# Fusing an attention block with a feed-forward block: values of two pairs of heads in one TensorE visit, and another order of accumulators at a group's start

## The chip, the cores and the metric

The kernel runs on one core of one Trainium2 chip. The metric is the device time of one execution in microseconds; lower is better. A second profiled execution, recorded by the hardware profiler, gives the rows shown here.

## The reference, cut to what matters

Attention over 4 batches, 8 heads, 768 positions and 64 dimensions per head, with a mask (the first 8 keys and the last 96), a distance bias, and a softmax; its output, 3072 rows of 512, goes through two dense layers with an ELU between them, all in float32:

```
scores = scale * q @ k.T + bias; scores = where(keep, scores, -1e9)
a = softmax(scores);  x = a @ v            # per head
h = x @ w_in;  g = where(h > 0, h, exp(min(h, 0)) - 1)
out = g @ w_out
```

## The kernel before

The 3072 rows are worked in 12 groups of 256 rows (two tiles of 128). Heads go in pairs: hp = 0 to 3 are the four pairs of a group, one head on each half of the 128 partitions. To keep float32 accuracy, most products are made of a rounded high part and a low rest (HI and LO), so that one product is three.

Groups 0 to 2 (n < GS = 3) work in an older way while weights arrive. From group 3 on ("later groups", about 204 us to the end) a group takes four **periods** of about 13.2 us, and TensorE's order in them is written by hand (`seq`, L70 on: operations with it go in that order and no other). One period is:

- two **ups** (L780): first-layer products of 24 matmuls each, 128x128 weights and 256 moving columns, into one PSUM bank per up. ScalarE and VectorE then compute the ELU in three steps (L708, L709, L710) and write `gg`, high and low.
- a **values visit** (L585): for one pair of heads of the *next* group, the product of the transposed probabilities `pt` with the values `rv`, into a tile `pv`: 8 products (6 in a sequence's first group) of 64 rows or columns. The trace has two records for each, so 16 or 12. ScalarE copies `pv` to `xh` high (L323), VectorE subtracts to get the low part (L331), 256 columns each.
- the **odd down** (L840): 21 second-layer products of the previous period's second up, into four accumulators a0 to a3. The second layer is worked by a seven-product scheme on 2 by 2 blocks, so a down has 7 products, each made of three.
- a **visit** (L562, L542): transposes of the next pair's probabilities into two banks `t` and `th` (t0, v0), and the scores of the pair after that into two banks (s0, s1).
- the **even down** (L840): 21 products of this period's first up.

Values of pair hp stand in period hp of the group before their own. `pv` may take bank v0 or t0, the same banks that the transposes of the visit need. The ups, the scores and so the ELU share the banks s0 and s1. `pt` of later groups has one buffer (pts: pt0), `rv` has two (part0, part1), each filled by a DMA on SyncE's queue, on which the first-layer weights `w0s` (four per period) are fetched too.

Between groups, the first accumulators of the new group need the four that the old one leaves, which ScalarE and VectorE combine (L856 to L862, tile `fin`). That happens in period 0 of the new group: odd down of the old group's last product, the visit, then the new group's first down (c = 0). Its 21 products run in the order raw high (a0, a0, a1), sums high (a1, a2, a2, a3), then the low ones.

The orders of ScalarE, VectorE and SyncE come from a planner (`Plan.order`) that places each operation by costs and due times.

Of the kernel before, what the change touches and what calls it, by code (L numbers as in the profile page):

```python
# [16 lines left out]
P = 128  # L17
# [5 lines left out]
NT = 2  # L23
W = NT * P
BIG = float(2 ** 100)

HI, LO = 0, 1
# [228 lines left out]
def pe(cols):  # L256
    return (("PE", cols * 0.47, False),)


def act(n, psum=False, extra=0.0):  # L260
    return (("ACT", (55 if psum else 97) + 0.834 * n + extra, False),)


def dve(n, fast=False, port=False):
    return (("DVE", (75 + 0.521 * n) if fast else (70 + 1.042 * n), fast or port),)
# [10 lines left out]
class Kernel:  # L276
# [191 lines left out]
    def pair(self, b, gi, hp, xh, xl, due, ahead, step, X):  # L468
        nc, p = self.nc, self.plan
# [7 lines left out]
        rv = rqv if rows else self.sb("rv", "rv", [P, VC])  # L477
# [29 lines left out]
        v32 = lambda: rv.t[:, nq if rows else 0:].rearrange("p (t j d) -> p t j d", t=2 * NT, j=2)  # L507
        k32 = lambda: rk.t
        sc = self.scale.t[:, hp:hp + 1]
        if rows:  # L510
# [5 lines left out]
            pv = self.bank("pv", "pv", [P, NT, P], X.get("pv"))  # L516
            self.pair32(b, hp, t0, q32, k32, v32, rqv, rk, pv, due, step, X)
            pvs = lambda: pv.t.rearrange("p i w -> p (i w)")
# [15 lines left out]
        st = self.sb("st", "st", [P, 3, 2 * NT])  # L534
        tiles = [(t0 + i, i * (NG + P)) + self.blocks(t0 + i) for i in range(NT)]
# [28 lines left out]
        def rest():  # L564
            pt = self.sb("pts", "pt", [P, 2, 2 * NT, P])
            d = due - 6000
            for x, tp in enumerate(tps):
                r = slice(64 * x, 64 * x + 64)
                if t0:
                    cut = [(slice(0, HK), slice(0, 4))]  # L570
                else:
                    cut = [(slice(0, kr), slice(2 * i + a0, 2 * i + 2)) for i, (_, _, _, a0, kr, _) in enumerate(tiles)]
                for rows, c in cut:
                    n = (c.stop - c.start) * 128
                    src = lambda tp=tp, rows=rows, c=c: tp.t.rearrange("p (j c) w -> p j c w", j=2)[rows, :, c]
                    out = lambda rows=rows, c=c, r=r: pt.t[rows, :, c, r]
                    p.add(act(n, True) + dve(n), lambda e, src=src, out=out: self.copy(e, out(), src()), [tp], [pt], d + 2 * x)
            pv = self.bank("pv", "pv", [P, NT, P])
            head = [slice(0, 64), slice(64, 128)]

            def values(e):
                for i, (_, _, _, a0, kr, _) in enumerate(tiles):
                    for a in range(a0, 2):
                        for j in range(2):
                            nc.tensor.matmul(pv.t[head[j], i], v32()[:kr, 2 * i + a, j], pt.t[:kr, j, 2 * i + a], start=a == a0, stop=a == 1)  # L585

            n = sum(2 - x[3] for x in tiles)
            self.after = [p.add((("PE", 160 + 216.0 * n, False),), values, [rv, pt], [pv], due, seq=due)]
            pvs = lambda: pv.t.rearrange("p i w -> p (i w)")
            p.add(act(W, True), lambda e: self.copy(e, xh.t[:, HI, hp], pvs()), [pv], [xh], due + 100)  # L590
            p.add(dve(W), lambda e: self.minus(e, xh.t[:, LO, hp], pvs(), xh.t[:, HI, hp]), [pv, xh], [xl], due + 200)

        self.prev = transposes, [v for x in prs for v in x], tps, 53.0 * 2 * sum(2 - x[3] for x in tiles), rest

# [190 lines left out]
    def moe7(self, rows, xh, xl, up_at, down_at):  # L785

        nc, p, N7, DM = self.nc, self.plan, self.NF7, self.DM
# [33 lines left out]
        def down(c, d, gg, low):  # L821
            a, b, ta, tb, k = self.seven[c]
            if not acc:
                acc.extend(self.bank(f"a{i}", "a", [P, 2, half], [s]) for i, s in enumerate(("o0", "o1", "h0", "h1")))
            far = slice(half, DM)
            near_, far_ = lambda w: lambda s: w.t[:, s, near], lambda w: lambda s: w.t[:, s, far]
            parts = ((A22, lambda s: tb.t[:, 2 * s + k], 0, 0), (A11, near_(a), 0, 1), (A12, near_(b), 1, 1), (S2, lambda s: ta.t[:, 2 * s + 1], 1, 0),
                     (S1, lambda s: ta.t[:, 2 * s], 2, 0), (S3, far_(a), 2, 1), (S4, far_(b), 3, 0))
            raw, sums = (0, 1, 2), (3, 4, 5, 6)
            high, rest = ((HI, HI), (HI, LO)), ((LO, HI),)  # L830
            if c < N7 - 1:
                todo = ((raw, high), (sums, high), (raw, rest), (sums, rest))
            else:
                todo = tuple((x, high + rest) for x in ((0, 1), (2, 3), (4, 5), (6,)))

            def products(e, ks, xs):
                for n in ks:
                    g, w, i, j = parts[n]
                    for x, s in xs:
                        nc.tensor.matmul(acc[i].t[:, j], gg.t[:, x, g], w(s), start=c == x == s == 0 and n in (0, 2, 4, 6),  # L840
                                         stop=c == N7 - 1 and x == LO and n in (1, 3, 5, 6))

            for m, (ks, xs) in enumerate(todo):
                need = [low[n] for n, kind in enumerate((raw, sums)) if rest[0] in xs and set(ks) & set(kind)]
                p.add(pe(len(xs) * len(ks) * half), lambda e, ks=ks, xs=xs: products(e, ks, xs), [a, b, ta, tb, gg] + need,
                      [acc[i] for i in sorted({parts[n][2] for n in ks})], d + 10 * m, seq=d + 10 * m)

        for c in range(N7):
            down(c, down_at[c], *up(c, up_at[c]))
        e = down_at[-1] - 20000  # L850
        fin = self.sb("fin", "fin", [P, 8, half], slots=["xh2"])
        first, second, spare, upper, lower = (p.tile(None, x, None) for x in ("first", "second", "spare", "upper", "lower"))
        f = lambda k, n=1: fin.t[:, k:k + n].rearrange("p i w -> p (i w)")
        v = nc.vector.tensor_tensor
# [12 lines left out]
    def build(self):  # L867
# [9 lines left out]
        at, start, wdue, dues = self.T0, {}, {}, []  # L877
# [9 lines left out]
            dues.append(d)  # L887
        self.start = start[self.GS]
        todo, self.held, self.parted, self.loads, self.asked = [], [], [], [], []
        self.prev, self.after = ((lambda: None), [], [], 0.0, (lambda: None)), []  # L890
        last = 0.0
        for n, (b, gi) in enumerate(groups):
# [5 lines left out]
            st = (hi - lo) / (4 * self.NP)  # L898
            for hp in range(self.NP):
# [5 lines left out]
                if n > self.GS:  # L905
                    ahead = start[self.GS] + self.PERIOD * (4 * (n - self.GS - 1) + hp - 2) + self.VISIT
                    d, st = ahead + self.AFTER, 600.0
# [30 lines left out]
        for _, f in sorted(todo, key=lambda x: x[0]):  # L938
# [18 lines left out]
    WARM, FILL = True, 60000.0  # L957
    SLOTS = {"rqv": ["rqv0"], "rk": ["rk0"], "qs": ["qs0"], "ks": ["ks0"], "rv": ["part0", "part1"],
             "s": ["s0", "s1"], "t": ["t0"], "th": ["v0"], "pv": ["v0", "t0"], "h": ["h0", "h1"], "S": ["s0", "s1"], "g7": ["io0", "io1", "io2", "io3"], "ring": ["w012", "w013", "w014", "w015"], "gg": ["gg0", "gg1"], "z": ["z0", "vd0"], "o0": ["o0"], "o1": ["o1"],
             "pr": ["pr0", "pr1", "pr2", "pr3"], "st": [f"st{i}" for i in range(6)], "pt": ["pt0", "pt1"], "pts": ["pt0"],  # L960
             "xh": ["xh0", "xh1", "xh2"], "e": ["z0", "e1"], "gh": ["gg0", "gg1", "gh2"],
             "gl": ["gl0", "gl1", "gl2"], "io": ["io0", "io1", "io2", "io3"], "part": ["part0", "part1", "vd0"]}

# [278 lines left out]
```

## Time and profile before

| | |
|---|---|
| time, median of 3 runs | 678.62 us (678.48 to 679.86) |
| profiled execution, own time | 678.11 us |
| its span | 676.3 us |
| TensorE busy | 660.5 us (98%) |
| VectorE busy | 516.9 us (76%) |
| ScalarE busy | 476.7 us (70%) |
| granted TensorE clock, mean | 0.996 |

The span is the time from the first to the last instruction. Busy time of TensorE counts overlapping matmuls once; a matmul's record is longer than the step from its start to the next one's start, so what one costs is read from the starts. In a timeline row the first number is the start in us from the span's start, the second the length of the merged row in us, and xN counts the instructions in it.

### The profile page before, as it was taken

To read this page: it belongs to the slowest core of one execution; us is meant where nothing else is said; L and a number is where in the kernel's file an instruction comes from. 1 tells how busy PE (TensorE), PEld (TensorE's weight loads), DVE (VectorE), ACT (ScalarE), POOL (GpSimd) and SP (SyncE) were. 2 spreads that over 40 slices of the span, in tenths; PEclk is the share of its full clock that TensorE was granted. 3 is DMA by queue.
4 is the path that set the end of the run, shared out by engine and by line. 5 is a ranking of instruction groups with operands and counts; after the bars stand their busy time and mean duration, and the time that the engine had idled before them with its cause. 6 is when DMAs were issued, how large, how long until landed. Compare 5 with 4: busy or idle time off the path is not lost.

```text
span 676.3 us, 15974 instructions
## 1 busy us (share of the span) xinstructions
PE 660.5 (98%) x5950; PEld 611.2 (90%) x5950; DVE 516.9 (76%) x1515; ACT 476.7 (70%) x1254; POOL 39.4 (6%) x65
## 2 busy tenths in 40 slices
PE   8999999999999999999999999999999999999995
PEld 6677888888888999999999999999999999999995
DVE  7999999999997677667767866866776777765653
ACT  7998888757786667766767766676777767664542
POOL 3143002011210000000000000000000000000000
PEclk9999999999999999999999999999999999999998
DMA  7837978510257665766676657656766765663841
GB/s 265 311 95 259 377 280 322 214 43 19 57 162 244 218 226 170 235 207 228 202 223 232 204 194 223 251 161 211 251 209 203 242 224 163 212 232 135 253 153 37
DMA packets 52233, 137.75 MB, mean 204 GB/s; under 512 B 5682, under 2 KB 18738, under 8 KB 52146
## 3 DMA queue, kind: packets, MB, share of 16 engines
q1 hardware_dynamic: 51856, 136.24, 59.7%
q8 instruction: 49, 0.80, 0.5%
q10 hardware_dynamic: 290, 0.39, 0.2%
q14 instruction: 38, 0.31, 0.1%
HBM read 119.84 MB, written 16.78 MB: 202 GB/s over the span
## 4 chain that ended last, share of the span: by engine, by line
PE 81%; DVE 11%; ACT 3%; DMA 2%; issue 1%; POOL 0%; DVEq 0%; POOLq 0%; SPq 0%
PE h L780 34%; PE a L840 28%; PE o L738 5%; PE pv L585 4%; PE s L542 3%; PE t L562 3%; DVE g L450 2%; DMA rqv<-in_qkv_dram 2%; PE s L666 2%; PE pv L700 1%; DVE gl L331 1%; PE t L683 1%; DVE e L710 1%; ACT pr L624 1%; DVE g L426 1%
## 5 line engine op out<-in xcount | busy, mean ns | idle before, releaser
L780 PE MATMUL h<-xh,w0s 128*128 128x256 f32 x1728 | 210.9, 282 | 0.0
L780 PEld LDWEIGHTS h<-xh,w0s 128*128 128x128 f32 x1728 | 207.3, 190 | 0.1
L840 PE MATMUL a<-w,gg 128*128 128x256 f32 x864 | 140.9, 278 | 0.0
L323 ACT CAST gg<-z 128x384 fp32r<-128x384 f32 (+1 forms) x144 | 81.4, 566 | 73.3 <-PE a L840 35.3
L710 DVE SCALAR_TENSOR_TENSOR z<-z,h 128x512 f32<-128x512 f32 x72 | 49.5, 688 | 106.3 <-ACT z L709 101.9
L840 PEld LDWEIGHTS a<-w,gg 128*128 128x128 f32 x864 | 119.5, 188 | 0.0
L624 ACT ACTIVATE pr<-pr,nmax 128x232 f32<-128x232 f32 (+1 forms) x192 | 90.7, 473 | 6.3 <-DVE nmax L622 6.2
L780 PEld LDWEIGHTS h<-xh,w 128*128 128x128 f32 x576 | 81.6, 189 | 8.8 <-issue 1.4
L331 DVE TENSOR_TENSOR gg<-z,gg 128x512 fp32r<-128x512 f32 (+1 forms) x144 | 84.5, 619 | 5.4 <-ACT gg L323 5.1
L780 PE MATMUL h<-xh,w 128*128 128x256 f32 x576 | 87.4, 284 | 0.1
L708 ACT ACTIVATE z<-h 128x512 f32<-128x512 f32 x72 | 43.0, 597 | 49.0 <-PE h L780 48.3
L811 DVE TENSOR_TENSOR z<-z 128x128 f32<-128x128 f32 (+1 forms) x216 | 72.3, 335 | 5.4
L622 DVE CUSTOM_DVE_ANT_0 pr<-s,tab 128x232 f32<-128x232 f32 (+1 forms) x192 | 62.8, 376 | 15.0 <-PE s L542 14.7
L840 PE MATMUL a<-ta,gg 128*128 128x256 f32 x432 | 72.1, 278 | 0.0
L738 PE MATMUL o<-w,gh 128*128 128x512 f32 x192 | 59.4, 402 | 1.6 <-DVE ob L765 1.2
L840 PEld LDWEIGHTS a<-ta,gg 128*128 128x128 f32 x432 | 59.7, 188 | 0.0
L840 PE MATMUL a<-tb,gg 128*128 128x256 f32 x216 | 53.5, 309 | 0.0
L709 ACT ACTIVATE z<-z 128x512 f32<-128x512 f32 x72 | 45.4, 631 | 2.1
L840 PEld LDWEIGHTS a<-tb,gg 128*128 128x128 f32 x216 | 34.5, 188 | 8.9 <-issue 5.3
L738 PEld LDWEIGHTS o<-w,gh 128*128 128x128 f32 x192 | 32.1, 189 | 6.6 <-ACT pr L624 1.6
L624 ACT ACTIVATION_READ_ACCUMULATOR pr<-pr,nmax 128x1 f32 x192 | 37.1, 193 | 0.0
L608 ACT ACTIVATE pr<-pr,st 128x232 f32<-128x232 f32 (+1 forms) x66 | 29.3, 468 | 10.4 <-DVE st L644 9.1
(122 smaller groups left out, 932.3 us busy)
## 6 DMA issues: line engine op xcount, KB each, us to landing
w0s<-kept SPq DMA_DIRECT2D x144, 512.0 KB, 5.1
rk<-in_qkv_dram SPq DMA_DIRECT2D x45, 184.0 KB, 2.5
bits<-in_w_in_dram SPq DMA_DIRECT2D x16, 512.0 KB, 7.3
bits<-in_w_out_dram SPq DMA_DIRECT2D x16, 512.0 KB, 9.5
kept<-w SPq DMA_DIRECT2D x16, 512.0 KB, 4.3
rv<-in_qkv_dram SPq DMA_DIRECT2D x32, 256.0 KB, 5.0
rqv<-in_qkv_dram SPq DMA_DIRECT2D x13, 384.0 KB, 3.7
rqv<-in_qkv_dram SPq DMA_DIRECT2D x34, 128.0 KB, 3.0
```

The costliest lines, as they stand in the source:

```text
L323: self.nc.scalar.copy(out, x)
L331: self.on(e).tensor_tensor(out, x, y, ALU.subtract)
L608: self.nc.scalar.activation(out, x, AF.Copy, scale=sc)
L622: p.add((("DVE", 158 + 1.042 * n, False),), lambda e: nc.vector.tensor_tensor_reduce(pr.t[:, lo:], st_()[:, lo:], tab, -(2.0 ** -(h + 1)), ...
L624: p.add(act(n, extra=200), lambda e: nc.scalar.activation(pr.t[:, lo:], pr.t[:, lo:], AF.Exp, bias=nm, scale=-1.0, accum_out=st.t[:, 0, i: ...
L708: p.add(act(n, True), lambda e: nc.scalar.activation(out(), hx(), AF.Relu, scale=-1.0), [h], [ex], due)
L709: p.add(act(n), lambda e: nc.scalar.activation(out(), out(), AF.Exp, scale=-1.0), [ex], [ex], due)
L710: p.add(dve(n), lambda e: nc.vector.scalar_tensor_tensor(out(), out(), -1.0, hx(), ALU.add, ALU.max), [h, ex], [ex], due)
L738: nc.tensor.matmul(acc[i].t, g.t[:, i * P:(i + 1) * P], w2.t[:, s], start=fc == f0 and n == 0 and s == HI, stop=fc == f1 - 1 and n == 1)
L780: self.nc.tensor.matmul(hx(), w1.t[:, s, cc * P:(cc + 1) * P], xh.t[:, x, cc], start=n == 0 and cc == 0, stop=n == 2 and cc == self.NCC - 1)
L811: tt = lambda e, out, x, y, op: self.on(e).tensor_tensor(out, x, y, op)
L840: nc.tensor.matmul(acc[i].t[:, j], gg.t[:, x, g], w(s), start=c == x == s == 0 and n in (0, 2, 4, 6), stop=c == N7 - 1 and x == LO and n i ...
```

## The change

Values of one pair (even hp) are held in a list until those of the next pair (odd hp) are ready; then both are computed in one visit, which has twice the products, in a `pv` tile twice as wide (a whole bank). The copy to `xh` and the subtraction handle both pairs at once, 512 columns each. The visit stands where the odd pair's stood, in periods 1 and 3; periods 0 and 2 have none. `pts` gets a second buffer, pt1, since two pairs' `pt` wait at once. In a group's first down (c = 0) the high sum products go a1, a3, a2, a2 in place of a1, a2, a2, a3; the counts are the same.

```
+            self.ready.append((v32, pt, rv))
+            if len(self.ready) < 2:
+                return
+            two, self.ready = self.ready, []
-            pv = self.bank("pv", "pv", [P, NT, P])
+            pv = self.bank("pv", "pv", [P, 2, NT, P])
...
+                for m, (v, x, _) in enumerate(two):
+                    for i, (_, _, _, a0, kr, _) in enumerate(tiles):
+                        for a in range(a0, 2):
+                            for j in range(2):
+                                nc.tensor.matmul(pv.t[head[j], m, i], v()[:kr, 2 * i + a, j], x.t[:kr, j, 2 * i + a], start=a == a0, stop=a == 1)
+
+            n = 2 * sum(2 - x[3] for x in tiles)
+            self.after = [p.add((("PE", 160 + 216.0 * n, False),), values, [y for x in two for y in x[1:]], [pv], due, seq=due)]
...
-            p.add(act(W, True), lambda e: self.copy(e, xh.t[:, HI, hp], pvs()), [pv], [xh], due + 100)
-            p.add(dve(W), lambda e: self.minus(e, xh.t[:, LO, hp], pvs(), xh.t[:, HI, hp]), [pv, xh], [xl], due + 200)
+            p.add(act(2 * W, True), lambda e: self.copy(e, both(HI), pvs()), [pv], [xh], due + 100)
+            p.add(dve(2 * W), lambda e: self.minus(e, both(LO), pvs(), both(HI)), [pv, xh], [xl], due + 200)
...
-            if c < N7 - 1:
+            if c == 0:
+                todo = (raw, high), ((3,), high), ((6,), high), ((4, 5), high), (raw, rest), (sums, rest)
+            elif c < N7 - 1:
...
-             ... "pts": ["pt0"],
+             ... "pts": ["pt0", "pt1"],
```

TensorE's order in period 1 of group 3 before: second up (two rows of 12), one values visit, odd down. The numbers after a name tell its instances apart.

```order
L780 MATMUL h_3254<-xh_2382,w0s_3075 128x256 x12
L780 MATMUL h_3254<-xh_2382,w0s_3092 128x256 x12
L585 MATMUL pv_3289<-pt_3177,rv_2815 64x128 x8
L840 MATMUL a_3169<-tb_2289,gg_3110 128x256 x2
L840 MATMUL a_3169<-w_108_629,gg_3110 128x256 x2
```

The same place after, with the values of the first pair (pt_2969) ahead of those of the second:

```order
L786 MATMUL h_3235<-xh_2382,w0s_3076 128x256 x12
L786 MATMUL h_3235<-xh_2382,w0s_3093 128x256 x12
L590 MATMUL pv_3275<-pt_2969,rv_2501 64x128 x8
L590 MATMUL pv_3275<-pt_3159,rv_2815 64x128 x8
L848 MATMUL a_3150<-tb_2289,gg_3110 128x256 x2
```

In period 2 after, the odd down follows the second up directly:

```order
L786 MATMUL h_3452<-xh_2382,w0s_3262 128x256 x12
L786 MATMUL h_3452<-xh_2382,w0s_3294 128x256 x12
L848 MATMUL a_3150<-tb_2467,gg_3364 128x256 x2
L848 MATMUL a_3150<-w_120_919,gg_3364 128x256 x2
L848 MATMUL a_3151<-w_429_1901,gg_3364 128x256 x2
```

What moved: half of the rows L585 by one period; nothing else on TensorE changes its place except at c = 0. There the high products of group 3 stood like this before (a_3169, 3170, 3181, 3182 are a0 to a3):

```order
L840 MATMUL a_3169<-tb_2289,gg_3086 128x256 x2
L840 MATMUL a_3169<-w_102_477,gg_3086 128x256 x2
L840 MATMUL a_3170<-w_303_1521,gg_3086 128x256 x2
L840 MATMUL a_3170<-ta_2276,gg_3086 128x256 x2
L840 MATMUL a_3181<-ta_2276,gg_3086 128x256 x2
L840 MATMUL a_3181<-w_102_477,gg_3086 128x256 x2
L840 MATMUL a_3182<-w_303_1521,gg_3086 128x256 x2
```

And after (a_3150, 3151, 3175, 3169 are a0 to a3):

```order
L848 MATMUL a_3150<-tb_2289,gg_3082 128x256 x2
L848 MATMUL a_3150<-w_102_477,gg_3082 128x256 x2
L848 MATMUL a_3151<-w_303_1521,gg_3082 128x256 x2
L848 MATMUL a_3151<-ta_2276,gg_3082 128x256 x2
L848 MATMUL a_3169<-w_303_1521,gg_3082 128x256 x2
L848 MATMUL a_3175<-ta_2276,gg_3082 128x256 x2
L848 MATMUL a_3175<-w_102_477,gg_3082 128x256 x2
```

What moved: the first use of a2 stands one row, two matmuls, later, and a3 comes before it. VectorE's order where the first of the eight boundaries between two later groups falls (from the second up's ELU on), before:

```order
L710 SCALAR_TENSOR_TENSOR z_3902<-z_3902,h_3854 128x512
L331 TENSOR_TENSOR xh_3917<-pv_3892,xh_3917 128x256
L331 TENSOR_TENSOR gg_3886<-z_3863,gg_3886 128x384
L857 TENSOR_TENSOR fin_3927<-a_3170,fin_3927 128x512
L331 TENSOR_TENSOR gg_3886<-z_3863,gg_3886 128x512
L858 TENSOR_TENSOR fin_3927<-a_3181,fin_3927 128x512
L811 TENSOR_TENSOR z_3902<-z_3902 128x128
L860 TENSOR_TENSOR fin_3927<-a_3181,fin_3927 128x256
L622 ISA pr_3990,nmax<-s_3943,tab_95 128x232
```

And after:

```order
L716 SCALAR_TENSOR_TENSOR z_3893<-z_3893,h_3851 128x512
L865 TENSOR_TENSOR fin_3906<-a_3151,fin_3906 128x512
L331 TENSOR_TENSOR gg_3880<-z_3856,gg_3880 128x384
L866 TENSOR_TENSOR fin_3906<-a_3175,fin_3906 128x512
L331 TENSOR_TENSOR gg_3880<-z_3856,gg_3880 128x512
L868 TENSOR_TENSOR fin_3906<-a_3175,fin_3906 128x256
L628 ISA pr_3973,nmax<-s_3922,tab_95 128x232
```

What moved: the subtraction for `xh` is gone from here and the 128-column step L811 stands later, so two fewer rows lie ahead of the last read of a2 (L860 before, L868 after). On SyncE's queue the two `rv` loads, which stood one in each period, stand together in every second one.

## Rows read from the trace of the kernel before

**Rows 1.** The page's part 1: busy us (share of the span) and instructions.

```profile
PE 660.5 (98%) x5950; PEld 611.2 (90%) x5950; DVE 516.9 (76%) x1515; ACT 476.7 (70%) x1254; POOL 39.4 (6%) x65
```

**Rows 2.** Timeline of TensorE: ups, values, odd down, first transpose (a period 2).

```profile
441.65 5.92 PE L780 MATMUL h<-xh,w0s 128*128 128x256 f32 x48
447.50 1.09 PE L585 MATMUL pv<-pt,rv 116*64 116x128 f32 x16
448.52 0.50 PE L840 MATMUL a<-tb,gg 128*128 128x256 f32 x2
...
451.19 0.27 PE L562 MATMUL t<-ident,pr 64*116 64x64 f32 x1
```

**Rows 3.** The same for a short values visit and the odd down's first row.

```profile
341.57 0.88 PE L585 MATMUL pv<-pt,rv 128*64 128x128 f32 x12
342.38 0.50 PE L840 MATMUL a<-tb,gg 128*128 128x256 f32 x2
```

**Rows 4.** The same for the very first values visit of the later groups.

```profile
210.27 0.40 PE L738 MATMUL o<-w,gl 128*128 128x512 f32 x1
210.60 1.10 PE L585 MATMUL pv<-pt,rv 116*64 116x128 f32 x16
212.79 0.27 PE L562 MATMUL t<-ident,pr 64*116 64x64 f32 x1 [1.10 <-DVE xh L331]
```

**Rows 5.** The same around the last values visit and into the last group.

```profile
612.13 5.62 PE L780 MATMUL h<-xh,w0s 128*128 128x256 f32 x48
617.67 1.09 PE L585 MATMUL pv<-pt,rv 116*64 116x128 f32 x16
618.70 0.50 PE L840 MATMUL a<-tb,gg 128*128 128x256 f32 x2
...
623.75 5.92 PE L780 MATMUL h<-xh,w0s 128*128 128x256 f32 x48
629.50 0.50 PE L840 MATMUL a<-tb,gg 128*128 128x256 f32 x3
...
631.88 3.04 PE L780 MATMUL h<-xh,w0s 128*128 128x256 f32 x24
```

**Rows 6.** Timeline of VectorE at the boundary between groups 3 and 4.

```profile
263.79 0.69 DVE L710 SCALAR_TENSOR_TENSOR z<-z,h 128x512 f32<-128x512 f32 x1 [1.02 <-ACT z L709]
264.39 0.42 DVE L331 TENSOR_TENSOR xh<-pv,xh 128x256 fp32r<-128x256 f32 x1
264.73 0.55 DVE L331 TENSOR_TENSOR gg<-z,gg 128x384 fp32r<-128x384 f32 x1
...
267.01 0.28 DVE L811 TENSOR_TENSOR z<-z 128x128 f32<-128x128 f32 x1
267.20 0.42 DVE L860 TENSOR_TENSOR fin<-a,fin 128x256 f32<-128x256 f32 x1
```

**Rows 7.** Timeline of TensorE there: first transpose, scores, first row of c = 0.

```profile
266.08 0.27 PE L562 MATMUL t<-ident,pr 64*116 64x64 f32 x1
...
266.56 0.91 PE L542 MATMUL s<-ks,qs 64*128 64x232 f32 x12
267.40 0.50 PE L840 MATMUL a<-tb,gg 128*128 128x256 f32 x2
```

**Rows 8.** VectorE at the boundary between groups 7 and 8.

```profile
479.18 0.42 DVE L860 TENSOR_TENSOR fin<-a,fin 128x256 f32<-128x256 f32 x1
```

**Rows 9.** TensorE's first row of c = 0 there.

```profile
478.86 0.50 PE L840 MATMUL a<-tb,gg 128*128 128x256 f32 x2
```

**Rows 10.** Instructions on tiles fin and pv: ns min/median/max of one.

```profile
L856 ACT COPY fin<-a x9: 571/587/592, 264.4 to 667.0; 128x512 f32<-128x512 f32 x9
L857 DVE TENSOR_TENSOR fin<-a,fin x9: 683/686/692, 265.2 to 667.8; 128x512 f32<-128x512 f32 x9
...
L323 ACT CAST xh<-pv x44: 350/354/390, 19.1 to 619.5; 128x256 fp32r<-128x256 f32 x44
```

**Rows 11.** Timeline of SyncE's queue (issues), one period.

```profile
276.77 0.33 SPq L505 DMA_DIRECT2D rv<-in_qkv_dram  x1
...
284.75 4.56 SPq L801 DMA_DIRECT2D w0s<-kept  x4
```

More of the change, by code (lines that the diff above doesn't have):

```diff
@@ L577, in rest @@
                     p.add(act(n, True) + dve(n), lambda e, src=src, out=out: self.copy(e, out(), src()), [tp], [pt], d + 2 * x)
-            pv = self.bank("pv", "pv", [P, NT, P])
+            self.ready.append((v32, pt, rv))
[3 more added lines that the diff above has]
+            pv = self.bank("pv", "pv", [P, 2, NT, P])
             head = [slice(0, 64), slice(64, 128)]
             def values(e):
[L582 to L589, printed above, removed]
-            p.add(act(W, True), lambda e: self.copy(e, xh.t[:, HI, hp], pvs()), [pv], [xh], due + 100)
-            p.add(dve(W), lambda e: self.minus(e, xh.t[:, LO, hp], pvs(), xh.t[:, HI, hp]), [pv, xh], [xl], due + 200)
+                for m, (v, x, _) in enumerate(two):
[5 more added lines that the diff above has]
+            self.after = [p.add((("PE", 160 + 216.0 * n, False),), values, [y for x in two for y in x[1:]], [pv], due, seq=due)]
+            pvs = lambda: pv.t.rearrange("p m i w -> p (m i w)")
+            both = lambda s: xh.t[:, s, hp - 1:hp + 1].rearrange("p m w -> p (m w)")
+            p.add(act(2 * W, True), lambda e: self.copy(e, both(HI), pvs()), [pv], [xh], due + 100)
+            p.add(dve(2 * W), lambda e: self.minus(e, both(LO), pvs(), both(HI)), [pv, xh], [xl], due + 200)
         self.prev = transposes, [v for x in prs for v in x], tps, 53.0 * 2 * sum(2 - x[3] for x in tiles), rest
@@ L889, in build @@
         todo, self.held, self.parted, self.loads, self.asked = [], [], [], [], []
+        self.ready = []
         self.prev, self.after = ((lambda: None), [], [], 0.0, (lambda: None)), []
@@ L959 @@
              "s": ["s0", "s1"], "t": ["t0"], "th": ["v0"], "pv": ["v0", "t0"], "h": ["h0", "h1"], "S": ["s0", "s1"], "g7": ["io0", "io1", "io2", "io3"], "ring": ["w012", "w013", "w014", "w015"], "gg": ["gg0", "gg1"], "z": ["z0", "vd0"], "o0": ["o0"], "o1": ["o1"],
-             "pr": ["pr0", "pr1", "pr2", "pr3"], "st": [f"st{i}" for i in range(6)], "pt": ["pt0", "pt1"], "pts": ["pt0"],
+             "pr": ["pr0", "pr1", "pr2", "pr3"], "st": [f"st{i}" for i in range(6)], "pt": ["pt0", "pt1"], "pts": ["pt0", "pt1"],
              "xh": ["xh0", "xh1", "xh2"], "e": ["z0", "e1"], "gh": ["gg0", "gg1", "gh2"],
```

## The prediction

> **What bounds the kernel now.** I read the page's part 1 first: TensorE is busy 98% of the span [rows 1], and the table's mean granted clock is 0.996, the higher level of 2.4 GHz nearly throughout, so from about 205 us on only what TensorE itself does, or waits for, can move the time. VectorE at 76% and ScalarE at 70% matter only where TensorE waits for them. Then I read TensorE's timeline of the later groups by starts. In the period shown the ups last from 441.65 to 447.50, the values visit to 448.52, the odd down to 451.19, and no row carries an idle time [rows 2]. I looked through all periods for one that waits; there is one, the very first, where the transposes waited 1.10 us for the low part of `xh` [rows 4]. So the question is what a values visit costs TensorE beyond its products, and what comes late when it goes.
>
> **A visit's fixed cost.** The visit of 16 records lasts 1.02 us (447.50 to 448.52) [rows 2], the one of 12 lasts 0.81 (341.57 to 342.38) [rows 3]. Four records make 0.21, so one makes 0.053, 16 make 0.85, 12 make 0.64, and 0.17 of either is fixed. Two more parts of the fixed cost stand in the neighbours. The 48 ups last 5.85 us where a values visit follows [rows 2] and 5.75 where the odd down follows directly (623.75 to 629.50) [rows 5]: 0.10 for switching in. The odd down behind a visit lasts 2.67 us up to the transposes [rows 2]; behind ups, and up to ups, it lasts 2.38 (629.50 to 631.88), which is 21 matmuls at 0.113 [rows 5]. Of that difference, 0.29, I give 0.10 to the switch into the transposes, which stays, by the 0.10 just found for the other switch. The other 0.19 is partly the switch back, partly that matmuls step more slowly there: two downs behind a visit, with nothing between, take 5.05 us (618.70 to 623.75), or 2.53 each, not 2.38 [rows 5]. So taking the visit away saves the odd down between 0.10 (its step stays slow, only the switch goes) and 0.19 (the step of 0.113 comes too).
>
> **The sum.** Groups 3 to 10 have 32 visits, four each; 16 go (periods 0 and 2) and 16 are doubled.
> - The first, at 210.60: from the last older matmul to the first transpose it is 2.52 us (210.27 to 212.79), wait included; without the visit one switch stays, taken at the 0.33 that leads into the visit (210.27 to 210.60) [rows 4]. That saves 2.19, and its 0.85 of products comes back in period 1: 1.34 net. It holds if VectorE has read the accumulators of the older down by then; transposes and scores, 1.32 long (266.08 to 267.40) [rows 7], stand in between and are the cover. Without it the saving falls to between 0 and 1.34.
> - Fifteen others: 0.10 + 1.02 + 0.10 = 1.22 saved where it goes, 0.85 added where it is doubled: 0.37 net. Four of them are the short kind, 0.10 + 0.81 + 0.10 - 0.64, also 0.37. Together 5.55.
> - The step of the odd downs in those 15 periods, 0 to 0.09 each. What sets it I can't see from the rows; the 48 ups too come in 5.54 (612.13 to 617.67) [rows 5] and in 5.85 [rows 2], both with the switch into a values visit. In groups 5, 7, 9 and in period 2 of group 3 the ups ahead step as in the last group, which is the nearest row, so I take 0.09 for these 7; for the 8 in even groups (the ups of 5.54 are one of theirs) no row has such ups ahead of a down, and I take half: 0.63 + 0.36 = 1.0.
>
> Here the page TensorE: Matmul & The Clock Gate of the Trainium skill (section Wait — 56ns, not 53.3ns?) would have it otherwise: it gives a warm matmul one step, its columns over 2.4 GHz plus some 2.5 ns, by my working 109 ns for 256 columns. By that rule no down could step more slowly than another. The trace disagrees with it: 113 ns in the last group, 120 on average in the pair of 5.05 us [rows 5].
>
> **What hides the rest.** ScalarE's copy for two pairs: 0.59 us for 512 columns against 0.35 for 256; VectorE's subtraction 0.69 [rows 10] against 0.42 [rows 6]. Both engines do less in all. In an odd period the transposes need the bank of `pv` back. At the boundary shown the subtraction ends at 264.81 [rows 6], 1.27 ahead of the transposes at 266.08 [rows 7]; the wider pair takes 0.24 + 0.27 of that and leaves 0.76. With that cover gone, each 0.1 that it comes late costs 1.6.
> In an even period the visit comes 1.22 to 1.31 sooner after the second up. Its scores need the bank that L710 reads until 264.48 [rows 6]. They start at 266.56 [rows 7], 2.08 later, so about 0.8 stays.
> SyncE: an `rv` load goes out right after its visit (276.77) and the next in the queue, the rest of a period's `w0s`, has a free place only at 284.75 [rows 11]. Two `rv` loads, queued behind a wait for the same visit, fit into those 8 us, and nothing behind them can be sent sooner.
>
> **The boundaries.** This is where the second edit works. Before, a2 is last read at 267.62 [rows 6], and its first use is the ninth matmul of c = 0 (a first step of 0.22 and seven of 0.113 behind 267.40 [rows 7]): 268.41, 0.79 later. So the order of accumulators by itself saves nothing: nothing waits. After, c = 0 comes 1.22 to 1.31 sooner. VectorE's chain shrinks by the subtraction (0.34, from 264.39 to 264.73) and by L811 (0.19, from 267.01 to 267.20), together 0.53 [rows 6]. 0.79 - 1.27 + 0.53 leaves 0.05, and the new order adds two matmuls, 0.23. At the two boundaries with short visits the last read ended at 479.60 [rows 8], 0.27 ahead of 479.87, the ninth matmul behind 478.86 [rows 9]. With 1.05 sooner, the same 0.53 and 0.23, nothing is left. So I cost the boundaries at 0.1 in all; if they have no cover, at up to 0.5 for each of 8, 4 us.
>
> Sum: 1.34 + 5.55 + 1.0 - 0.1 = 7.8 us off the profiled execution's 678.11, which is 670.3. The median of the runs is 0.51 above that execution, so 670.8 is predicted.
>
> **Rivals.**
> - Steps stay slow in all odd downs, so the last term is nothing: 6.8 us, 671.8. For it: the pair behind a visit kept its slow step to the end, so a step once set may stay [rows 5]. Against: the last group's direct down, in the same rows. The page TensorE: Matmul & The Clock Gate of the Trainium skill, with one step for all (the same section), comes to the same time.
> - Steps turn worse. The ups of the even groups go from 5.75 to 5.85 with the new neighbours (16 periods, 1.6 us) and even downs lose the 0.09 that odd ones may win (25 of them, 2.2 us): 7.8 - 3.8 = 4.0, 674.6. For it: the same code shows 5.54 and 5.85 [rows 2, 5]. The mirror of it, ups at 5.54, would give some 4 us more, 666.8.
> - The boundaries wait 0.5 each, since covers of 0 to 0.3 hold only while both chains run as I reckon: 4.0 more, 674.8.
> - Slower: the scores of the 16 even periods wait for the second up's ELU. The gain of 7.8 is lost at 0.49 of waiting in each. With 0.8 of cover the ELU would have to end 1.3 later than now; at 2 us later the sum is 16 x 1.2 - 7.8 = 11 us slower, 690. For it: ScalarE loses 1.2 us of each even period, in which it also has the same exponentials. Against: VectorE waited 1.02 for ScalarE just there [rows 6] and ScalarE has one copy less ahead.
>
> **How the numbers follow.** Forecast 0.60, own range 669.6 to 671.4; slow steps 0.18; worse steps 0.07, their mirror 0.03; boundaries 0.08; slower 0.04. Forecast and slow steps make 0.78; reaching up to 673.8, into the cases of waits and worse steps at half their price, and down to 668.8, holds some 0.82. A change of 0.2% is 1.36 us, about what a measurement of this kernel can tell from none. All cases but the last clear it by far; a mix of waits and worse steps could end within it. Faster 0.92, the same 0.04, slower 0.04.
>
> **What would show it.** Right: 16 values visits, of about 1.87 us (1.5 for short ones), none in even periods; even periods about 1.2 shorter and odd ones 0.85 longer; no wait of 1.1 us near 211; odd downs of 2.47 to the transposes behind ups. Wrong: an idle time on TensorE ahead of the scores, the transposes or c = 0; ups or downs with another step than before; a doubled visit that costs twice the single one, since then 0.17 of each 0.37 comes back.

## The result, and the profile after

| | before | after |
|---|---|---|
| median in the shared runs | 678.55 us (676.84 to 679.86) | 671.75 us (671.12 to 672.64) |
| profiled execution, own time | 678.11 us | 671.63 us |
| its span | 676.3 us | 669.8 us |
| last older down to the end of TensorE's work | 460.93 us | 454.20 us |

The ratio is 0.9891, with a 95% interval of 0.9866 to 0.9915: faster, by 6.8 us where 7.8 was forecast (670.8; range 668.8 to 673.8). The last row of the table is what the sum was about. It runs from the start of the last older down (207.76 before, 207.69 after) to the end of the last stretch, which lasts 7.30 us in both. What lies ahead of it varies between executions (below), so experiments are compared by this stretch, called "the later stage".

Part 1 of the page after, columns as in [rows 1], and then one row of busy time by window under its heading, with the granted clock as PEclk:

```profile
PE 655.5 (98%) x5950; PEld 610.5 (91%) x5950; DVE 517.6 (77%) x1504; ACT 477.9 (71%) x1233; POOL 39.6 (6%) x65
```

```profile
core 0: us, PE busy (x) PEld busy (x) DVE busy (x) ACT busy (x) POOL busy (x), PEclk, DMA share, GB/s
205.00:662.00 457.00, 456.89 (x4534) 443.35 (x4533) 319.38 (x917) 312.76 (x761) 0.00 (x0) 1.00 0.63 210
```

TensorE still bounds the kernel, at the higher clock (1.00) throughout the later stage. Its timeline after, at the places of [rows 2 to 5]:

```profile
210.21 0.40 PE L744 MATMUL o<-w,gl 128*128 128x512 f32 x1
210.53 0.27 PE L562 MATMUL t<-ident,pr 64*116 64x64 f32 x1
...
211.86 0.51 PE L848 MATMUL a<-tb,gg 128*128 128x256 f32 x2
...
254.91 5.82 PE L786 MATMUL h<-xh,w0s 128*128 128x256 f32 x48
260.57 0.52 PE L848 MATMUL a<-tb,gg 128*128 128x256 f32 x3
...
263.14 0.27 PE L562 MATMUL t<-ident,pr 64*116 64x64 f32 x1
...
263.61 0.91 PE L542 MATMUL s<-ks,qs 64*128 64x232 f32 x12
264.45 0.50 PE L848 MATMUL a<-tb,gg 128*128 128x256 f32 x2
...
307.09 5.92 PE L786 MATMUL h<-xh,w0s 128*128 128x256 f32 x48
312.84 0.50 PE L848 MATMUL a<-tb,gg 128*128 128x256 f32 x3
...
315.32 0.27 PE L562 MATMUL t<-ident,pr 64*128 64x64 f32 x1
...
423.06 5.92 PE L786 MATMUL h<-xh,w0s 128*128 128x256 f32 x48
428.90 1.97 PE L590 MATMUL pv<-pt,rv 116*64 116x128 f32 x32
430.80 0.50 PE L848 MATMUL a<-tb,gg 128*128 128x256 f32 x2
```

Read by the starts: the first transpose stands 0.32 behind the last older matmul, with no wait, where 2.52 us lay before [rows 4]. A doubled visit takes 1.90 (428.90 to 430.80). In an even period the odd down follows the ups directly (a "direct" down). In an even group (here 4) the ups take 5.66 and the down 2.57; in an odd one (here 5) they take 5.75 and 2.48. One even period stands apart, period 2 of group 8, with 5.45 and 2.475.

VectorE after, at the boundary between groups 3 and 4, then its last reads of a doubled `pv` and, at the next boundary, of a2:

```profile
262.06 0.69 DVE L716 SCALAR_TENSOR_TENSOR z<-z,h 128x512 f32<-128x512 f32 x1 [1.03 <-PE a L848]
262.67 0.68 DVE L865 TENSOR_TENSOR fin<-a,fin 128x512 f32<-128x512 f32 x1
...
275.76 0.68 DVE L331 TENSOR_TENSOR xh<-pv,xh 128x512 fp32r<-128x512 f32 x1
...
317.21 0.42 DVE L868 TENSOR_TENSOR fin<-a,fin 128x256 f32<-128x256 f32 x1
```

L716 ends at 262.75, 0.86 ahead of the scores at 263.61. The subtraction that followed it before [rows 6] is gone from here.

### The profile page after: what moved, and what is told of

Its sections match the earlier page's. It is cut to its first block, busy times and chain, and to the rows that moved or that the text cites. A ratio compares the mean times of both kernels' runs of the same rounds, so it can differ in the third digit from the quotient of the medians.

```text
span 669.8 us, 15954 instructions
## 1 busy us (share of the span) xinstructions
PE 655.5 (98%) x5950; PEld 610.5 (91%) x5950; DVE 517.6 (77%) x1504; ACT 477.9 (71%) x1233; POOL 39.6 (6%) x65
## 4 chain that ended last, share of the span: by engine, by line
PE 86%; DVE 8%; ACT 3%; DMA 1%; issue 1%; POOL 0%; POOLq 0%; DVEq 0%; SPq 0%
PE h L786 37%; PE a L848 27%; PE o L744 7%; PE pv L590 4%; PE s L542 3%; PE t L562 3%; PE pv L706 1%; PE t L689 1%; ACT pr L630 1%; DMA rqv<-in_qkv_dram 1%; PE s L672 1%; DVE g L450 1%; DVE gl L331 1%; DVE g L426 1%; DVE e L716 1%
## 5 line engine op out<-in xcount | busy, mean ns | idle before, releaser
L716 DVE SCALAR_TENSOR_TENSOR z<-z,h 128x512 f32<-128x512 f32 x72 | 49.5, 688 | 104.0 <-ACT z L715 95.5
L848 PE MATMUL a<-tb,gg 128*128 128x256 f32 x216 | 52.0, 302 | 0.0
L614 ACT ACTIVATE pr<-pr,st 128x232 f32<-128x232 f32 (+1 forms) x76 | 32.8, 466 | 10.2 <-DVE st L650 8.6
L323 ACT COPY pt<-t 116x512 f32<-116x512 f32 (+2 forms) x80 | 34.8, 442 | 3.2 <-PE t L689 0.9
```

What stands on the lines that cost most here:

```text
L323: self.nc.scalar.copy(out, x)
L614: self.nc.scalar.activation(out, x, AF.Copy, scale=sc)
L716: p.add(dve(n), lambda e: nc.vector.scalar_tensor_tensor(out(), out(), -1.0, hx(), ALU.add, ALU.max), [h, ex], [ex], due)
```

## The experiments

Ratios are against runs of the kernel before on the same chip. Diffs are against the changed kernel, if nothing else is said.

**1. The old order of accumulators at c = 0.**

```
-            if c == 0:
-                todo = (raw, high), ((3,), high), ((6,), high), ((4, 5), high), (raw, rest), (sums, rest)
-            elif c < N7 - 1:
+            if c < N7 - 1:
```

> The changed kernel with the old order of accumulators at c = 0; the merged values stay. Theory (the new order is cover that the merging makes necessary): in the trace of the changed kernel the first use of a2 starts 0.12 after its last read at best and is late by 0.05 at worst at the boundaries; two matmuls sooner (0.23) it waits 0.11 to 0.28 at each of 8, in all 1.2 to 1.5 us, so about 673.0, and TensorE's downs of c = 0 grow from 2.49 to about 2.65. Rival (the order is worth nothing, VectorE simply comes sooner): 671.8 within 0.3, downs of c = 0 as before.

Measured: 671.92 us, ratio 0.9906 (0.9880 to 0.9931): by the time not to be told from the changed kernel. In the trace the later stage lasts 455.64 us, 1.44 more than 454.20, and its downs 184.33 against 182.90. This execution had only reached the stage 1.19 us sooner. TensorE and VectorE at the boundary between groups 4 and 5, old order:

```profile
315.45 0.51 PE L846 MATMUL a<-tb,gg 128*128 128x256 f32 x2
315.79 0.63 PE L846 MATMUL a<-w,gg 128*128 128x256 f32 x4
316.26 0.91 PE L846 MATMUL a<-ta,gg 128*128 128x256 f32 x4
317.01 0.63 PE L846 MATMUL a<-w,gg 128*128 128x256 f32 x4
```

```profile
316.13 0.42 DVE L866 TENSOR_TENSOR fin<-a,fin 128x256 f32<-128x256 f32 x1
```

and the changed kernel there:

```profile
317.35 0.40 PE L848 MATMUL a<-ta,gg 128*128 128x256 f32 x2
317.58 0.39 PE L848 MATMUL a<-w,gg 128*128 128x256 f32 x2
317.81 0.43 PE L848 MATMUL a<-ta,gg 128*128 128x256 f32 x2
318.08 0.40 PE L848 MATMUL a<-w,gg 128*128 128x256 f32 x2
```

In the old order the row of four from 316.26 takes 0.75 us to the next start, not 0.47: its third matmul is a2's first, and the read ends at 316.55. All seven boundaries between later groups show it (0.11 to 0.26 each, 1.24 in sum). In the new order a3 stands there (317.58), and a2's first matmul starts at 317.81, after the read that ends at 317.63 (the last row of VectorE after, above); its row lasts 0.27 instead of 0.24. So the second edit is worth 1.2 to 1.4 us, but only together with the first. No idle time is printed for these waits, since the records of earlier matmuls overlap them; only the starts show them.

**2. The new order alone, in the kernel before** (the same lines, added to it).

> The kernel before with the new order of accumulators alone. Theory: nothing waited there (cover of 0.3 to 0.8 us), so no change, 678.5 within 0.5, same starts in the timeline of TensorE. Rival (the order is part of the gain by itself): at least 1 us faster, 677.5 or less.

Measured: 678.86 us, ratio 1.0004 (0.9993 to 1.0015); later stage 460.93, as before to the hundredth. Nothing waited for a2 as long as the visits stood in even periods.

**3. Two visits in place of the doubled one**, one between the ups of the odd period and one behind them; `pv`, copy and subtraction stay wide.

```
...
-            self.after = [p.add((("PE", 160 + 216.0 * n, False),), values, [y for x in two for y in x[1:]], [pv], due, seq=due)]
+            self.after = [p.add((("PE", 160 + 216.0 * n, False),), lambda e, m=m: values(e, m), list(two[m][1:]), [pv], s, seq=s)
+                          for m, s in enumerate((due - 5720.0, due))]
```

> The changed kernel, but the even pair's values stand in a visit of their own between the two ups of the odd period; the odd pair's stay where they are; one wide eviction as in the changed kernel. Theory (each visit has a fixed cost of 0.37: 0.10 to switch in, 0.17 within, 0.10 to switch back): 16 visits more than the changed kernel, 16 x 0.37 = 5.9 us, 677.7; even periods stay as short as in the changed kernel. Rival A (only the 0.17 within a visit counts, the switches are hidden between ups): 16 x 0.17 = 2.7, 674.5. Rival B (what pays is the wide eviction and the shorter even period, not the count of visits): 671.8.

Measured: 678.25 us, ratio 0.9989 (0.9970 to 1.0007); later stage 460.19, 5.99 more than the changed kernel. TensorE:

```profile
214.93 3.03 PE L787 MATMUL h<-xh,w0s 128*128 128x256 f32 x24
217.89 1.09 PE L590 MATMUL pv<-pt,rv 116*64 116x128 f32 x16
218.92 3.14 PE L787 MATMUL h<-xh,w0s 128*128 128x256 f32 x24
221.99 1.09 PE L590 MATMUL pv<-pt,rv 116*64 116x128 f32 x16
```

Each visit takes 1.03 again, and the two halves of the ups 2.96 and 3.07, 0.19 more than 5.84 in one piece. So 16 visits more cost 0.37 each, as forecast, 0.35 of it within the visits and in the ups beside them, though the ELU and the copies of this kernel are those of the changed one. It is the number of visits that pays.

**4. All four pairs in one visit**, in period 3, for groups 5 to 11 (more buffers for `pt` and `rv` in free tiles, two `pv` tiles).

```
+            many = 4 if X.get("four") else 2
-            if len(self.ready) < 2:
+            if len(self.ready) < many:
...
+            for k in range(many // 2):
+                pv = self.bank("pv", "pv", [P, 2, NT, P])
```

> All four pairs of a group in one visit in period 3, as two wide tiles in the two banks, for the seven groups from 5 on; group 4 as in the changed kernel. The additional buffers are ones that are idle in these groups. Theory (a visit's fixed cost, whatever its size): 7 visits fewer, 7 x 0.37 = 2.6, and 0.09 each for the odd downs of period 1 in groups 5, 7 and 9 (0.3): 2.9 less than the changed kernel, 668.9. Rival (covers run out: the transposes behind the fourfold visit wait for the second tile's eviction, which has 0.8 us of cover now, or the values' loads come late): waits in period 3 that take back what goes, 671.8 or more.

Measured: 668.23 us (668.16 to 668.46), ratio 0.9847 (0.9826 to 0.9869); later stage 451.05.

```profile
393.39 5.61 PE L790 MATMUL h<-xh,w0s 128*128 128x256 f32 x48
398.93 3.71 PE L595 MATMUL pv<-pt,rv 116*64 116x128 f32 x64
402.57 0.50 PE L852 MATMUL a<-tb,gg 128*128 128x256 f32 x2
```

The visit takes 3.64. Seven visits fewer, at 0.34 (below) to 0.37 (run 3) each, make 2.4 to 2.6 of the 3.15 us gained; the rest is other steps, as here: these 48 ups take 5.54, those of this group in the changed kernel 5.75.

**5. The names of the two later `xh` buffers exchanged**, meant to ask whether a group's step goes by its `xh`.

```
-  ... ["xh0", "xh1"] if n > self.GS else None ...
+  ... [("xh1", "xh0", "xh2", "xh1")[n] if n < 4 else ("xh0", "xh1")[n % 2]] ...
```

> The changed kernel with the two buffers of xh exchanged between odd and even groups; nothing else. It asks what sets the step of ups and direct odd downs. In the changed kernel 48 ups ahead of a direct odd down take 5.75 to 5.76 and that down 2.47 in the odd groups 3, 5, 7, 9, against 5.66 and 2.57 in the even ones. Theory (the step goes by the buffer that the ups read): the two change places, 5.76 and 2.47 in groups 4, 6, 8, 10 and 5.66 and 2.57 in 3, 5, 7, 9; the time stays within 0.5 of 671.8. Rival (it goes by something else that alternates or by what runs before): the pattern stays with the groups.

Measured: 672.11 us, ratio 0.9886 (0.9844 to 0.9928), every stretch as in the changed kernel but for 0.135 us in the last. It told nothing on the question: all names were exchanged, each got the other's address, and no tile moved. Run 9 asks again.

**6. The first two pairs in visits of their own**, the others merged.

```
-            if len(self.ready) < 2:
+            many = 1 if X.get("alone") and hp < 2 else 2
+            if len(self.ready) < many:
...
```

> The changed kernel, but the first two pairs of group 4 keep a visit each, in periods 0 and 1 of group 3, as before the change. Theory (the very first visit cost its fixed part and a wait of 1.10 us, and both come back): from the last older matmul to the first transpose 2.5 us instead of 0.3, in all 1.3 us more than the changed kernel, 673.1. Rival (the wait near 211 us would have been taken up later anyway): 0.4 more, 672.1, or a shorter wait elsewhere.

Measured: 672.93 us, ratio 0.9898 (0.9856 to 0.9941); later stage 455.44, 1.23 more than the changed kernel (forecast for that term: 1.34). The wait of [rows 4] is back:

```profile
210.83 0.40 PE L745 MATMUL o<-w,gl 128*128 128x512 f32 x1
211.16 1.09 PE L591 MATMUL pv<-pt,rv 116*64 116x128 f32 x16
213.36 0.27 PE L562 MATMUL t<-ident,pr 64*116 64x64 f32 x1 [1.11 <-DVE xh L331]
```

**7 and 8. The kernel with four pairs and the changed kernel again**, on one chip.

> The kernel with four pairs in one visit once more, beside the changed kernel on the same chip. Theory: 668.2 within 0.5, so 3 to 4 us less than the changed kernel. Rival (the first measurement caught a favourable set of steps of the matmuls): nearer to 670.

> The changed kernel itself once more, for the comparison with the one of four pairs: 671.8 within 0.5; the same kernel's fixed timings from 211 us on, with what differs coming from ahead of that.

Measured: 668.29 us (ratio 0.9839, 0.9807 to 0.9872) and 672.16 us (0.9886, 0.9854 to 0.9918). The later stages repeat: 450.95 and 454.22. The changed kernel's profiled execution took 675.52 us. In it TensorE stood idle for 2.39 us (to 26.68), and from 27.5 to 30.9 us its granted clock was 0.50, the lower level of 1.2 GHz; the execution of 671.63 us shows neither there. The first transposes stand here, 4.47 us later than at 210.53:

```profile
215.00 0.27 PE L562 MATMUL t<-ident,pr 64*116 64x64 f32 x1
```

**9. The `xh` buffers really exchanged:** groups 3, 5, 7, 9, 11 get the place that 4, 6, 8, 10 had, and the other way about.

```
-  ... ["xh0", "xh1"] if n > self.GS else None ...
+  ... [("xh0", "xh1")[n % 2]] if n >= self.GS else None ...
```

> The changed kernel, with the `xh` buffers of the later groups exchanged in on-chip memory: groups 3, 5, 7, 9 have the buffer that groups 4, 6, 8, 10 had, and the other way about (the names in the earlier experiment were exchanged, too, but each name got the other's place, so there nothing moved). Theory A, that the step of a stretch of first-layer matmuls, and of the down behind it, goes by where `xh` lies: in even periods odd groups would now show ups of 5.66 us and direct odd downs of 2.57, even groups 5.75 and 2.47, the total within 0.3 us of the changed kernel. Theory B, that it goes by something else (what stood ahead, the weights' buffers): each stretch from group 4 on is as in the changed kernel, within 0.01. Under both the time is that of the changed kernel, 671.8, within 0.5%.

Measured: 675.37 us, ratio 0.9955 (0.9926 to 0.9985). The later stage is shorter than the changed kernel's, 453.57; the stage ahead of it, where TensorE's order changes too when group 3 has another buffer, ended 4.9 us later in this execution. TensorE there:

```profile
204.26 8.48 PE L786 MATMUL h<-xh,w0s 128*128 128x256 f32 x48 [0.82 <-DVE nmax L628]
212.57 0.62 PE L744 MATMUL o<-w,gh 128*128 128x512 f32 x2
```

It had stood idle for 1.54 and 0.82 us just before, and from 203.3 to 210.2 us its granted clock was 0.51, the lower level; these 48 ups took 8.31 us, in the changed kernel 5.74 (201.95 to 207.69). The five of the eight executions that took 675.3 to 677.4 us have a mean granted clock of 0.990 to 0.994, the three of 672.4 to 672.7 us 0.995 or 0.996. TensorE in group 5:

```profile
311.87 5.82 PE L786 MATMUL h<-xh,w0s 128*128 128x256 f32 x48
317.53 0.52 PE L848 MATMUL a<-tb,gg 128*128 128x256 f32 x3
...
320.10 0.27 PE L562 MATMUL t<-ident,pr 64*128 64x64 f32 x1
```

Ups 5.66 and down 2.57, where the changed kernel has 5.75 and 2.48. Every group changes with its buffer: on the first place the ups of even periods take 5.75 to 5.76 and the direct down 2.47, on the second 5.65 to 5.66 and 2.57, or 5.45 and 2.475. Theory A holds in the later stage; the time it gave did not, by the waits and the clock ahead of that stage.

**10 and 11. All tiles 32 bytes further; and the two `xh` buffers at the same offset.**

```
+        self.pad = self.const("pad", [P, 8])
```

and, for the second, with the floats to be left free ahead of a buffer:

```
+PADS = {"xh0": 48, "xh1": 80}
...
+                    pad = PADS.pop(v.slot, 0)
+                    if pad:
+                        self.m.tile([P, pad], F32, tag="pad" + v.slot, name="pad" + v.slot)
```

> The changed kernel with 32 bytes more per partition ahead of all tiles, so that every tile of on-chip memory (weights, xh, gg, probabilities) lies 32 bytes further. The run before showed that a group's step goes by which of two places its `xh` has; this one asks whether it is the place itself, counted from a boundary, or how the tiles lie to each other. Theory A, distances between tiles decide: every stretch of the later stage as in the changed kernel, within 0.02 us; from the first transposes to the last stretch 444.06 us. Theory B, the place counted from a boundary of 64 bytes decides (xh and gg began 32 bytes off one, now on one): ups of all groups in 5.45 to 5.55 and direct downs of 2.38 to 2.475; about 0.2 us in each of 34 stretches of ups, 6 to 7 us less, 665.

> The changed kernel with 192 bytes per partition left free ahead of the one `xh` buffer and 320 ahead of the other: the first moves by 192 bytes, what follows the second by 512, and both buffers then lie 32 bytes behind a multiple of 512 (before, 352 and 32). In the runs so far groups on the first buffer show ups of 5.75 in even periods, 5.84 in odd ones, those on the second 5.45 to 5.66 and 5.54 to 5.75. Theory A, the offset within 512 bytes (against the weights' 96) sets the step: no group shows 5.75 in even periods or 5.84 in odd ones; groups 3, 5, 7, 9 and 11 step as those on the second buffer, 0.1 to 0.3 less in each of some 16 stretches, 1.5 to 5 us less from the first transposes to the last stretch than the changed kernel's 444.06; the time 667 to 670.5. Theory B, something else of the two places: the pattern by group stays, 444.06 within 0.3, the time 671.8.

Measured: 672.91 us, ratio 0.9913 (0.9881 to 0.9946), later stage 454.22 with the changed kernel's pattern; and 667.90 us, ratio 0.9828 (0.9790 to 0.9865), later stage 450.47, of which the ups gave 4.6 (195.78 against 200.40) and the downs took 0.8. Group 5 in run 11:

```profile
308.25 5.62 PE L788 MATMUL h<-xh,w0s 128*128 128x256 f32 x48
313.71 0.50 PE L850 MATMUL a<-tb,gg 128*128 128x256 f32 x3
...
316.18 0.27 PE L564 MATMUL t<-ident,pr 64*128 64x64 f32 x1
```

5.46 and 2.47. No stretch of ups in any group takes 5.75 in an even period or 5.84 in an odd one any more. So an offset from a boundary of 64 bytes is out, and run 10 speaks for the distance between `xh` and other tiles; to which, and whether a coarser boundary counts, these two runs can't tell. The offset of a group's own `xh` isn't all: groups 4 and 8, whose buffer kept its offset within 512, went from 5.65 or 5.66 to 5.45 in period 0 as well, so something is passed on from the group ahead, or other distances count.

**12. Four pairs and the same offset together.**

> Both steps that gained, in one kernel: all four pairs of a group in one visit (as in the run of 668.2), and both `xh` buffers 32 bytes behind a multiple of 512 (as in the run of 667.9). Theory, the two add: from the first transposes to the last stretch the four pairs took 440.91 us, of which the places of xh should take 3.7 off as they did from 444.06 (to 440.33): 437.2; the time 664.5, ratio 0.979. Rival, that the step is set by the whole neighbourhood, so that a change of what stands ahead of an up undoes it: some groups fall back to 5.75 to 5.84 for their ups, and 439 to 441 stays; 667 to 668.

Measured: 666.00 us (664.95 to 667.44), ratio 0.9810 (0.9793 to 0.9827); later stage 448.58. From the first transposes to the last stretch it took 438.15: 2.76 less than with four pairs alone, where the theory took 3.7 off (437.2) and the rival left 439 to 441. So the two add for the most part, and no direct ups fall back to 5.75. The last stretch itself took 7.585 instead of 7.30; why, no run shows. This is the fastest version, 5.75 us below the changed kernel.

## Why the prediction was right, and what was mis-sized

The later stage became 6.73 us shorter: values 3.58, ups 1.25, downs 1.88, transposes and scores unchanged. Step by step:

- **The first visit.** Forecast 2.19 less and 0.85 back, 1.34. Measured 2.19 (5.03 to 2.84 us from the last older down to the first transposes) and 0.87 back, 1.32. Run 6 gives it back alone, 1.23.
- **Fifteen other visits.** Forecast 0.37 each. The doubled visit takes 1.90 where two took 1.02 each, so 0.15 was fixed within it, not 0.17. The ups became 0.089 shorter in each of the 15 even periods and the downs 0.10: 0.34 each, 5.1 for 5.55. Run 3 shows that it is the visits, at 0.37. That the 0.10 for switching in came out near 0.089 is in part luck: it was read from groups 7 and 11, which have the same `xh` buffer (run 9 shows why that matters). Groups 10 and 11, on different ones, show 5.54 with a visit and 5.75 without [rows 5], which would have given the wrong sign.
- **The step of the odd downs.** Forecast 0.63 for odd groups and period 2 of group 3, 0.36 for even groups. Measured: 7 downs became 0.195 shorter, which is switch and 0.095 of step, 0.67; the 8 in even groups became 0.10 shorter, the switch alone. The 0.36, taken as half for want of a row, was nothing. The rival of worse steps and its mirror didn't come: ups that still lead into a visit take 5.54, 5.75 or 5.85 in the same places as before.
- **What no term held.** Three downs (the first of group 3, two of group 8) became 0.09 longer each, and one up of the last group too: 0.36 in all. The first of group 3 is the one even down of 25 for which the rival of worse steps did come.
- **Boundaries.** Forecast 0.1 of waiting; measured 0.03, at 317.81. The covers, from the end of a2's last read to its first matmul, are near the reckoning: 0.25 to 0.35 at five boundaries (0.28 forecast), 0.19 and 0.28 at the two with short visits (nothing forecast). But the reckoning took a cover as free to its end, and it isn't: in run 1, where a2 is waited for, its first matmul starts 0.145 behind the end of the read at all seven boundaries, and the step behind that takes some 0.08 more. In the changed kernel 0.25 shows no wait and 0.19 cost the 0.03. So about 0.22 of a cover is used up, an estimate from these rows, and at the covers of 0.25 some 0.03 was left.
- **Other covers.** The scores have 0.86 in the even period shown (0.8 forecast), and the subtraction ends at 276.44, 0.82 ahead of the transposes at 277.26 (0.76). The slower rival, scores waiting for the ELU, didn't occur.

The mechanism was right; the terms that were too large are the step in even groups (0.33 over) and the fixed part of a visit with its switches (0.45 over); 0.36 of longer stretches was missing. With them 7.8 becomes 6.7. The rival "slow steps" gave the time (671.8), but not for its reason: in odd groups the fast step came, as forecast.

What the step hangs on, which the prediction could not see, runs 9 to 11 showed in part: the place of the group's `xh`. Why some groups on the second place take 118 ns and others 113, and what passes the step on to the next stretch, stays open.

## What to carry to other kernels

Where one engine is busy throughout, count how often it changes between kinds of product, and price one change from the starts on both sides; merging small visits pays per visit, and the covers they gave to others must be reckoned along (here the new order of accumulators kept 1.3 us that the merging would have lost). Compare variants by the stretch that the edit touches when another stretch varies more than the effect. And look at where operands lie: moving one buffer of `xh` by 192 bytes, and what lies behind the other by 512, gave more than half of what the merge gave.

## What the runs showed that was not expected

- Matmuls of the same shape, 128x256, step by 113, 118 or 120 ns, steady through a stretch and the same in two profiled executions of one program, at a granted clock of 1.00. For 48 ups that is 5.45 to 5.85 us, the longest with the switch into a visit. The one step per shape that the page TensorE: Matmul & The Clock Gate of the Trainium skill gives for warm matmuls back to back (section Wait — 56ns, not 53.3ns?) does not show here, where each matmul has a weight load of its own.
- That step changes when `xh` moves against the other tiles (runs 9 and 11, in run 11 by 3.7 us in all), and does not when all tiles move together by 32 bytes (run 10).
- A wait of 0.1 to 0.3 us for a PSUM bank leaves no idle time in the rows of TensorE (run 1).
- The later stage repeats within 0.2 us between executions of one program (454.20, 454.22 and, with no tile moved, 454.36), while what lies ahead of it varied by 4.5 us (207.69 and 212.16), in the longer one with an idle time of 2.39 us and then 3.4 us at the lower clock.
